# Splitting the first attention units of each layer across key ranges, in a four-layer attention kernel on one Trainium2 core

## The chip, the cores and the metric

The kernel runs on one NeuronCore of a Trainium2 chip. The metric is the device time of one launch in microseconds (us). A single-core run has no second die to be compared with, so the granted TensorE clock that each run lists (its mean over the run, as a share of full speed) is used here to tell like runs from unlike ones; all runs below carry the state "fast".

## The reference

Four layers of self-attention with residual, without a feed-forward part; layers 0 and 2 use the weights A, layers 1 and 3 the weights B. Each layer's keys and values need the output of the whole layer below.

```python
def _A_ref(x, wqkv, wo):                      # _B_ref is the same
    B, S, D = x.shape                         # 1, 2048, 448
    H = 16; Dh = D // H                       # 16 heads of 28
    qkv = (x @ wqkv).reshape(B, S, 3, H, Dh).transpose(2, 0, 3, 1, 4)
    q, k, v = qkv[0], qkv[1], qkv[2]
    p = _softmax(jnp.einsum("bhqd,bhkd->bhqk", q, k) * Dh ** -0.5, axis=-1)
    o = jnp.einsum("bhqk,bhkd->bhqd", p, v)
    return o.transpose(0, 2, 1, 3).reshape(B, S, D) @ wo

x = A_x
x = x + _A_ref(_layernorm(x), A_wqkv, A_wo)
x = x + _B_ref(_layernorm(x), B_wqkv, B_wo)
x = x + _A_ref(_layernorm(x), A_wqkv, A_wo)
x = x + _B_ref(_layernorm(x), B_wqkv, B_wo)
```

## The kernel before

The 2048 rows are four chunks (`NQC`) of four 128-row tiles (`TPC`). A **unit** is one chunk of 512 queries times one group of four heads; a layer has 16 units. A unit has 16 **steps**, one for each key tile: two score tiles (each two matmuls into a 128x1024 slot of PSUM, the buffers that matmuls write to), two exponentials on ScalarE, and one PV accumulation (the probabilities times V, added up over the key tiles).

```python
for step in range(nstep):                 # 256 steps a layer
    mk_exp(2 * step)                      # ScalarE, 128x1024
    mk_scores(2 * step + 2)               # TensorE
    js.step(W1)                           # up to 440 ns of filler
    mk_exp(2 * step + 1)
    mk_scores(2 * step + 3)
    mk_pv(step)
    js.step(W2)                           # up to 260 ns of filler
    if kt == NT - 1: unit_end(u)          # normalise, transpose
```

Everything else is **filler**: chains of small stages (`ln_chain`, `k_chain`, `v_chain`, `q_chain`, the end of a unit, the output projection) that a scheduler, working when the program is built, puts between the attention matmuls by priority and budget. The order in which it puts them is the order of each engine's instruction list. `js.force` emits the rest of a chain at once.

A softmax needs a bound on its scores. Here a per-head bound `beta` is added through spare rows of Q; it needs the maximum of |k|^2 over **all** keys:

```python
def beta_finish(L):
    V(tensor_reduce(kmax2, kmaxp[:, :, :], max))         # all four chunks
    V(tensor_scalar(betav, kmax2, -0.505, c0v, mult, add))
...
# after the last step of a layer
ctx["act_free"] = True
js.flush(fill=lambda: pe_fill(NFBND))      # the rest, one piece at a time
beta_finish(L + 1); q_fixup(L + 1, 0); qmask(...)
```

So no score of layer L+1 can start before the last chunk of layer L is projected, added to x, normalised, and turned into K and its maximum. `pe_fill` issues matmuls whose results are not used.

Of the kernel before, what the change touches and what calls it, by code (L numbers as in the profile page):

```python
# [8 lines left out]
ALU = mybir.AluOpType  # L9
# [210 lines left out]
def build_kernel(nc, A_x, A_wqkv, A_wo, B_x, B_wqkv, B_wo, out,  # L220
                 n_layers=4, c0=50.0, markers=False, NWARM=40, NFPRO=1, NFBND=1, W1=440.0, W2=260.0):
# [18 lines left out]
    with es:  # L240
# [19 lines left out]
        accS = sb("accS", [128, 2, QC], F32)  # L260
        On = sb("On", [128, 2, QC], BF16)
# [11 lines left out]
        kmaxp = sb("kmaxp", [128, G, NQC], F32)  # L273
        kmax2 = sb("kmax2", [128, G], F32)
        betav = sb("betav", [128, G], F32)
# [6 lines left out]
        augrow = sb("augrow", [1, 128], BF16)  # L282
        maskv = sb("maskv", [128, 4], F32)
# [88 lines left out]
        def late_init():  # L372
# [14 lines left out]
        P(lambda g_: g_.affine_select(btmp[:, 0, :], ones_bf[:, 0:128], [[-Dh, 128]], ALU.is_ge, 0.0,  # L387
                                      base=Dh * GW, channel_multiplier=1), reads=["ones_bf", "augrow"], writes=["btmp0"])
        P(lambda g_: g_.affine_select(btmp[:, 1, :], btmp[:, 0, :], [[Dh, 128]], ALU.is_ge, 0.0,
                                      base=Dh - 1 - Dh * GW, channel_multiplier=-1), reads=["btmp0"], writes=["btmp1"])  # L390
        P(lambda g_: g_.affine_select(bsel[:, :], btmp[:, 1, :], [[-1, 128]], ALU.is_ge, 0.0,
                                      base=GW + 3, channel_multiplier=0), reads=["btmp1"], writes=["bsel"])
# [5 lines left out]
        P(lambda g_: g_.tensor_scalar(avec[:, :], maug[:, :], -0.505, None, ALU.mult), reads=["maug"], writes=["avec"])  # L398
        P(lambda g_: g_.affine_select(mtmp2[:, 0:4], ones_f[:, 0:4], [[-Dh, 4]], ALU.is_ge, 0.0,
# [5 lines left out]
        P(lambda g_: g_.tensor_tensor(maskv[:, :], mtmp2[:, 0:4], mtmp2[:, 4:8], ALU.add),  # L405
          reads=["mt2a", "mt2b"], writes=["maskv"])
# [94 lines left out]
        def k_chain(L, c, g):  # L501
# [43 lines left out]
            def bq():  # L545
                b = stt["b"]
                sl2 = pb_alloc()
                T(lambda t_: t_.matmul(PB[:, sl2, :], bsel[:, :], sqb[:, b, :], start=True, stop=True),  # L548
                  reads=[("sq", b), "bsel"], writes=[("PB", sl2)])
                pfree("sq", b)  # L550

                def post():
                    V(lambda v_: v_.tensor_reduce(kmaxp[:, g, c:c + 1], PB[:, sl2, :], AX.X, ALU.max),  # L553
                      reads=[("PB", sl2)], writes=[("kmaxp", g, c)])
                    pb_free(sl2)
                return post
            return [(a1, 432, 0, ("bank",)), (a2, 432, 0, ()), (a3, 216, 2, ("sq",)), (bq, 216, 0, ("bank",))]

        def v_chain(L, tt):
# [17 lines left out]
            def a2():  # L577
# [10 lines left out]
                def post():  # L588
                    ev_copy(VA[:, tt, :].rearrange("p (h e) -> p h e", e=HP)[:, :, 0:Dh],
                            PB[:, sl, 0:D].rearrange("p (h d) -> p h d", d=Dh),  # L590
                            reads=[("PB", sl), ("VAone", nb)], writes=[("VA", nb, tt)], prefer_act=False)
                    pb_free(sl)
# [3 lines left out]
        def q_chain(L, c, g, with_beta):  # L596
            ws = L % 2
            cs = c % 2
# [8 lines left out]
            def a1():  # L607
                sl = stt["sl"] = pb_alloc()

                def f(t_):  # L610
                    t_.matmul(PB[:, sl, :], augrow[0:1, :], zrow[0:1, :], start=True, stop=False)  # L611
                    return mm(t_, sl, 0, False)
                T(f, reads=rd + ["augrow", "zrow"], writes=[("PB", sl)])
# [9 lines left out]
            def a3():  # L623
# [3 lines left out]
                def post():  # L627
                    bq_ = stt["bq"] = palloc("qtb")
                    if with_beta:
                        V(lambda v_: v_.tensor_scalar(qtb[:, bq_, :], PB[:, sl, :], betav[:, g:g + 1], None, ALU.add),  # L630
                          reads=[("PB", sl), "betav"], writes=[("qtb", bq_)])
                    else:
                        ev_copy(qtb[:, bq_, :], PB[:, sl, :], reads=[("PB", sl)], writes=[("qtb", bq_)])
                    b = stt["b"] = palloc("sq")
                    if ctx["act_free"]:
                        A(lambda a_: a_.activation(sqb[:, b, :], PB[:, sl, :], ACTF.Square),
                          reads=[("PB", sl)], writes=[("sq", b)])
                    else:
                        V(lambda v_: v_.tensor_tensor(sqb[:, b, :], PB[:, sl, :], qtb[:, bq_, :], ALU.mult),
# [21 lines left out]
        def beta_finish(L):  # L661
            V(lambda v_: v_.tensor_reduce(kmax2[:, :], kmaxp[:, :, :], AX.X, ALU.max),
              reads=[("kmaxp", g, c) for g in range(G) for c in range(NQC)], writes=["kmax2"])
            V(lambda v_: v_.tensor_scalar(betav[:, :], kmax2[:, :], -0.505, c0v[:, 0:1], ALU.mult, ALU.add),
              reads=["kmax2", "c0v"], writes=["betav"])

        def q_fixup(L, g):
            V(lambda v_: v_.tensor_scalar(QT[:, 0, g, :], QT[:, 0, g, :], betav[:, g:g + 1], None, ALU.add),
              reads=[("QT", 0, g), "betav"], writes=[("QT", 0, g)])
# [6 lines left out]
        def spawn_chunk(L, c, prio, vjit, vprio):  # L676
            key = (L, c)
            chunk_cnt[key] = 0

            def done():  # L680
                chunk_cnt[key] += 1
                if chunk_cnt[key] == TPC:
                    for g in range(G):
                        js.add(k_chain(L, c, g), delay=1, prio=prio)
                    for j in range(TPC):
                        js.add(v_chain(L, c * TPC + j), delay=1, prio=vprio + j,
                               tag=("jit", "v", L, c * TPC + j) if vjit else "crit")
# [4 lines left out]
        for c in range(NQC):  # L692
            done = spawn_chunk(0, c, prio=c, vjit=(c >= 2), vprio=c * TPC)
            for tt in range(c * TPC, (c + 1) * TPC):
                js.add(ln_chain(0, tt, done), prio=c)
        js.flush(fill=lambda: pe_fill(NFPRO))
        marker([("KT", 0, 3, NQC - 1)])
        js.add(q_chain(0, 0, 0, False))
        js.flush(fill=lambda: pe_fill(NFPRO))
        beta_finish(0)  # L700
        q_fixup(0, 0)
        qmask(0, 0, 0)
        marker([("QTm", 0, 3)])

        STEPS_PER_UNIT = NT
        SPQ = G * STEPS_PER_UNIT
        UNITS = [(qc, g) for qc in range(NQC) for g in range(G)]
        NSTEP_L = len(UNITS) * STEPS_PER_UNIT
        gt = {"tile": 0, "unit": 0}
# [5 lines left out]
        def layer(L):  # L715
# [5 lines left out]
            assert sorted(pbfree["free"]) == [0, 1, 2, 3], pbfree  # L721
            pbfree["free"] = [2, 3]
            ctx["act_free"] = False
            tb = gt["tile"]
            ub0 = gt["unit"]
            ntile = 2 * NSTEP_L
            lstart = js.now
            lend = lstart + NSTEP_L

            def tinfo(ti):  # L730
                step, hp = divmod(ti, 2)
                u, kt = divmod(step, STEPS_PER_UNIT)
                return u, kt, hp

            def mk_scores(ti):
                u, kt, hp = tinfo(ti)
                qc, g = UNITS[u]
                slot = (tb + ti) % 2
                qb = (ub0 + u) % 2
                if kt == 0 and hp == 0 and u > 0:  # L740
                    js.force(lambda ch: ch.tag == ("jit", "qm", L, u))
# [18 lines left out]
            def mk_pv(step):  # L760
                ti0 = 2 * step
                u, kt, _ = tinfo(ti0)
                qc, g = UNITS[u]
                aslot = (ub0 + u) % 2
                if u == 0:
                    js.force(lambda ch: ch.tag == ("jit", "v", L, kt))

                def f(t_):
                    ins = None
                    for i in range(4):  # L770
# [5 lines left out]
                                        start=(kt == 0), stop=(kt == NT - 1), tile_position=(0, 32 * i))  # L776
# [4 lines left out]
            def unit_end(u):  # L781
                qc, g = UNITS[u]
                aslot = (ub0 + u) % 2
                ub = cnt["ub"] % 2
                cnt["ub"] += 1
                ob = qc % 2
                stt = {}

                def s1():
                    V(lambda v_: v_.tensor_copy(accS[:, ub, :], PB[:, aslot, :]), reads=[("PB", aslot)], writes=[("accS", ub)])  # L790
                    if ctx["act_free"]:
                        pbfree["free"].append(aslot)
# [50 lines left out]
                js.add([(s1, 0, 1, ()), (s2a, 250, 0, ("bank",)), (s2, 250, 1, ()), (s3, 300, 0, ("bank",))], delay=1, prio=js.now)  # L843

            def chunk_tail(qc):
                ob = qc % 2
                c = qc
                done = None if last else spawn_chunk(L + 1, c, prio=lend, vjit=(c == NQC - 1), vprio=lend + c * TPC)
                for j in range(TPC):
# [14 lines left out]
                    def t1(j=j, tt=tt, stt=stt):  # L864
# [10 lines left out]
                        def post():  # L875
# [6 lines left out]
                            else:  # L882
                                js.add(ln_chain(L + 1, tt, done), delay=1, prio=lend)
                        return post
                    js.add([(t0, 380, 1, ("bank",)), (t1, 380, 0, ())], delay=1 + j, prio=js.now + 8)

            for c in range(1, NQC):
                for g in range(G):
                    js.add(q_chain(L, c, g, True), delay=(c - 1) * SPQ + SPQ // 2 + 2 * g, prio=lstart + c * SPQ - 8,
                           tag=("jit", "q", L, c, g))  # L890
            if not last:
                for g in range(G):
                    js.add(q_chain(L + 1, 0, g, False), delay=(NQC - 1) * SPQ + SPQ // 2 + 2 * g, prio=lend - 4)
            if L == 0:
                if n_layers > 1:
                    js.add([(late_init, 0, 0, ())], delay=STEPS_PER_UNIT + 2, tag=("jit", "late"))
                for g in range(1, G):
# [106 lines left out]
```

## Time and profile before

| | before |
|---|---|
| median of runs | 2132.2 us (2129.76 to 2145.55) |
| span of the profiled run | 2128.0 us, mean clock 0.991 |
| ScalarE busy | 92% of the span |
| first exponential starts at | 73.26 us |
| three holes between layers | 28.2 + 33.5 + 27.0 = 88.7 us |
| after the last exponential | 16.5 us |

The page of the kernel before gives busy time by engine, and by group: engine and operation, out <- in, count | busy us, mean ns of one | idle us of the engine just before, and what ended it. PE stands for TensorE's matmuls, PEld for its weight loads, DVE for VectorE, ACT for ScalarE and POOL for GpSimd; L757 is line 757 of the kernel.

```profile
PE 1920.2 (90%) x10474; PEld 574.1 (27%) x10474; DVE 603.3 (28%) x1211; ACT 1967.3 (92%) x2143; POOL 68.4 (3%) x161
...
L757 ACT ACTIVATE PT<-SC 128x1024 bf16<-128x1024 f32 x2048 | 1910.3, 1073 | 55.9 <-PE SC L747 49.4
```

The exponentials fill 1910 of 2128 us. A mean of 1073 ns is not their pace: neighbours overlap, and most start 904 to 921 ns after the one before (917 ns is used as the pitch below). The timeline of ScalarE around the first layer boundary (start, duration, what, count, idle before and its releaser) shows a hole in them:

```profile
558.97 7.55 ACT L757 ACTIVATE PT<-SC 128x1024 bf16<-128x1024 f32 x8
570.15 0.60 ACT L324 ACTIVATE OTn<-PB 128x512 bf16<-128x512 bf16 x1 [3.63 <-PE PB L832]
581.04 1.57 ACT L324 ACTIVATE xnT<-PB 112x512 bf16<-112x512 bf16 x3 [10.30 <-PE PB L487]
...
594.74 5.61 ACT L757 ACTIVATE PT<-SC 128x1024 bf16<-128x1024 f32 x6 [4.04 <-PE SC L747]
```

The exponentials stop at 566.52 and start again at 594.74. The windows view says what each engine did in such a stretch (columns: window, length, then busy us and instruction count of PE, PEld, DVE, ACT and POOL, the granted clock, DMA share, GB/s). Here are the first hole, the second layer, and the second hole:

```profile
566.52:594.74 28.22, 21.05 (x102) 9.27 (x103) 13.15 (x31) 7.11 (x13) 3.43 (x8) 0.94 0.00 1
594.74:1081.28 486.54, 448.54 (x2490) 131.78 (x2488) 143.21 (x283) 477.94 (x512) 9.47 (x24) 1.00 0.00 1
1081.28:1114.74 33.46, 27.35 (x102) 10.83 (x103) 13.43 (x31) 7.15 (x14) 3.43 (x8) 0.74 0.00 0
```

ScalarE, the bottleneck, works 7 us of a hole. TensorE shows 21 us there, but 11 us of that are fill matmuls. The second hole has the same matmuls; it is longer, and the clock fell to 0.74 in it (0.50 from 1095.08 to 1112.14 us).

### The profile page before, as it was taken

The numbers are of one execution on the slowest core, as the hardware profiler recorded it, in microseconds if no ns is written. First come the engines' busy times: TensorE is split into PE (matmuls) and PEld (weight loads), VectorE is DVE, ScalarE is ACT, GpSimd is POOL, SyncE is SP. The second block draws the span as 40 slices with busy tenths as digits, with TensorE's granted clock in tenths as the row PEclk, the third lists the DMA queues.
The fourth block names the chain that finished last, engine by engine and source line by source line (L and its number), as shares of the span: only waits on it lengthen the run. The fifth ranks groups of instructions, "written<-read, shape, count | busy, mean of one in ns | idle before, by whom it ended". The sixth has DMA issues, their size and how long they took to land.

```text
span 2128.0 us, 24673 instructions
## 1 busy us (share of the span) xinstructions
PE 1920.2 (90%) x10474; PEld 574.1 (27%) x10474; DVE 603.3 (28%) x1211; ACT 1967.3 (92%) x2143; POOL 68.4 (3%) x161
## 2 busy tenths in 40 slices
PE   9998999999889898999988999898998888989887
PEld 4322323223222232323222223232322222222222
DVE  5322423323222232423321234232423121212111
ACT  5699999999689999999959999999996999999996
POOL 4000000000000000000000000000000000000000
PEclk9999999999999999999989999999999999999999
DMA  3000000000000000000000000000000000000000
GB/s 88 8 1 1 1 1 1 1 1 1 1 1 1 1 1 1 1 1 1 1 0 1 1 1 1 1 1 1 1 1 0 1 1 9 1 9 1 9 1 9
DMA packets 6606, 8.46 MB, mean 4 GB/s; under 512 B 608, under 2 KB 5600, under 8 KB 6496
## 3 DMA queue, kind: packets, MB, share of 16 engines
q1 hardware_dynamic: 4384, 5.05, 0.9%
q0 software_dynamic: 2112, 1.84, 0.6%
q8 instruction: 82, 1.34, 0.3%
q14 instruction: 28, 0.23, 0.0%
HBM read 5.05 MB, written 1.84 MB: 3 GB/s over the span
## 4 chain that ended last, share of the span: by engine, by line
ACT 58%; PE 37%; DVE 4%; issue 1%; POOL 0%; DVEq 0%; POOLq 0%
ACT PT L757 57%; PE SC L747 16%; PE PB L774 5%; PE PB L510 3%; PE PB L604 3%; DVE On L818 2%; PE SC L332 2%; PE PB L832 1%; PE PB L810 1%; PE PB L517 1%; PE PB L611 1%; DVE rz L815 1%; PE PB L583 1%; PE PB L548 1%; DVE x_sb L876 0%
## 5 line engine op out<-in xcount | busy, mean ns | idle before, releaser
L757 ACT ACTIVATE PT<-SC 128x1024 bf16<-128x1024 f32 x2048 | 1910.3, 1073 | 55.9 <-PE SC L747 49.4
L747 PE MATMUL SC<-QTm,KT 128*128 128x512 bf16 x4096 | 1238.1, 384 | 138.0 <-ACT PT L757 114.4
L747 PEld LDWEIGHTS SC<-QTm,KT 128*128 128x128 bf16 x4096 | 264.4, 98 | 739.8 <-ACT PT L757 640.5
L774 PE MATMUL PB<-PT,VA 128*32 128x512 bf16 x4096 | 410.0, 390 | 5.9 <-ACT PT L757 3.6
L774 PEld LDWEIGHTS PB<-PT,VA 128*32 128x32 bf16 x4096 | 105.2, 92 | 441.3 <-issue 432.4
L790 DVE COPY accS<-PB 128x512 f32<-128x512 f32 x64 | 44.3, 692 | 631.2 <-PE PB L774 631.2
L604 PE MATMUL PB<-xnT,wq 112*112 112x512 bf16 x256 | 92.2, 402 | 0.0
L510 PE MATMUL PB<-xnT,wq 112*112 112x512 bf16 x256 | 85.5, 412 | 0.0
L332 PE MATMUL SC<-ones_bf,ident 128*128 128x512 bf16 x234 | 79.4, 407 | 1.9 <-POOL ident L380 1.9
L876 DVE TENSOR_TENSOR x_sb<-PB,x_sb 128x448 f32<-128x448 f32 x64 | 39.6, 625 | 136.1 <-PE PB L870 136.1
L326 DVE CAST VA<-PB 128x448 bf16<-128x448 f32 x64 | 39.9, 624 | 132.2 <-PE PB L583 132.2
L630 DVE TENSOR_SCALAR qtb<-PB,betav 128x512 bf16<-128x512 f32 x51 | 38.3, 751 | 122.7 <-PE PB L604 122.7
L673 DVE TENSOR_SCALAR QTm<-QT,maskv 128x512 bf16<-128x512 bf16 x256 | 72.8, 348 | 0.1
L815 DVE RECIPROCAL rz<-PB 128x16 f32<-128x16 f32 x64 | 16.5, 258 | 175.9 <-PE PB L810 175.9
L468 POOL TENSOR_SCALAR ve<-mv 128x1 f32<-128x1 f32 x64 | 15.2, 237 | 1544.5 <-DVE mv L467 1544.4
L553 DVE TENSOR_REDUCE kmaxp<-PB 128x1 f32<-128x512 f32 x64 | 42.6, 688 | 74.9 <-PE PB L548 74.9
L832 PE MATMUL PB<-ident,On 128*128 128x128 bf16 x256 | 25.6, 223 | 42.2 <-DVE On L818 42.2
L653 DVE SCALAR_TENSOR_TENSOR QT<-PB,avec,qtb 128x512 bf16<-128x512 f32 x64 | 48.1, 751 | 55.2 <-PE PB L648 54.0
L324 ACT ACTIVATE xnT<-PB 112x512 bf16<-112x512 bf16 x28 | 15.2, 597 | 39.6 <-PE PB L487 39.6
L326 DVE CAST KT<-PB 128x512 bf16<-128x512 f32 x36 | 24.9, 692 | 86.1 <-PE PB L510 86.1
L818 DVE TENSOR_TENSOR On<-PB,rz 128x512 bf16<-128x512 f32 x64 | 44.2, 691 | 2.2
L604 PEld LDWEIGHTS PB<-xnT,wq 112*112 112x112 bf16 x256 | 32.9, 129 | 42.1 <-issue 29.0
(73 smaller groups left out, 824.3 us busy)
## 6 DMA issues: line engine op xcount, KB each, us to landing
out_dram<-x_sb POOLq DMA_DIRECT2D x4, 448.0 KB, 4.3
wq<-in_A_wqkv_dram SPq DMA_DIRECT2D x1, 1176.0 KB, 7.8
wq<-in_B_wqkv_dram SPq DMA_DIRECT2D x1, 1176.0 KB, 13.5
PT<-in_A_x_dram SPq DMA_DIRECT2D x2, 448.0 KB, 6.1
OTn<-in_A_x_dram SPq DMA_DIRECT2D x2, 448.0 KB, 9.4
wop<-in_A_wo_dram SPq DMA_DIRECT2D x16, 24.5 KB
wop<-in_B_wo_dram SPq DMA_DIRECT2D x16, 24.5 KB
```

Of the source, the lines that this page charges most:

```text
L326: V(lambda v_: v_.tensor_copy(out_ap, in_ap), reads=reads, writes=writes)
L332: T(lambda t_, r_=r_: t_.matmul(SC[:, r_ % 2, (r_ // 2 % 2) * 512:(r_ // 2 % 2 + 1) * 512], ident[:, :], ones_bf[:, :], start=True, stop=T ...
L510: return t_.matmul(PB[0:GW, sl, :], wq[ws][:, cc, D + g * GW:D + (g + 1) * GW], xnT[:, cc, c * QC:(c + 1) * QC], start=False, stop=last_)
L604: return t_.matmul(PB[0:GW, sl, :], wq[ws][:, cc, g * GW:(g + 1) * GW], xnT[:, cc, c * QC:(c + 1) * QC], start=False, stop=last_)
L653: V(lambda v_: v_.scalar_tensor_tensor(QT[:, cs, g, :], PB[:, sl2, :], avec[:, 0:1], qtb[:, bq_, :], ALU.mult, ALU.add), reads=[("PB", sl2 ...
L673: V(lambda v_, i=i: v_.tensor_scalar(QTm[:, qb, i, :], QT[:, cs, g, :], maskv[:, i:i + 1], None, ALU.mult), reads=[("QT", cs, g)] + maskk, ...
L747: ins = t_.matmul(SC[:, slot, j * 512:(j + 1) * 512], KT[:, g, kt * 128:(kt + 1) * 128], QTm[:, qb, i, :], start=True, stop=True)
L757: A(lambda a_: a_.activation(PT[:, pslot, :], SC[:, slot, :], ACTF.Exp, scale=SCALE), reads=[("SC", slot)], writes=[("PT", pslot)], name=" ...
L774: ins = t_.matmul(PB[32 * i:32 * i + 32, aslot, :], VA[:, kt, h * HP:(h + 1) * HP], PT[:, pslot, j * 512:(j + 1) * 512], start=(kt == 0), ...
L790: V(lambda v_: v_.tensor_copy(accS[:, ub, :], PB[:, aslot, :]), reads=[("PB", aslot)], writes=[("accS", ub)])
L818: V(lambda v_: v_.tensor_tensor(On[:, ub, :].rearrange("p (a e) -> p a e", e=HP), PB[:, sl, :].rearrange("p (a e) -> p a e", e=HP), rz[:, ...
L832: ins = t_.transpose(pv_[:, s_ * 128:(s_ + 1) * 128], On[:, ub, s_ * 128:(s_ + 1) * 128], ident[:, :])
```

## The change

Its intent: start the next layer without its last key chunk. Four things belong to it.

1. The first four units of a layer (query chunk 0, all four head groups) run keys 0-11 first (parts A, 12 steps each), then keys 12-15 (parts B). The accumulator of part A is parked in SBUF and added at the end of B. The last chunk thus has 48 steps (96 exponentials, about 88 us) to arrive in.
2. `beta` comes from the first three chunks. If the last chunk has a larger key, its K gets a lowering term through a second set of spare rows, and its V a compensating factor `fv` (a small exponential on ScalarE).
3. The flush between layers goes; the last unit's end becomes filler, and so do the projection, layer norm and K of the last chunk, tagged `("late", L + 1)` and forced only before the first part B.
4. In the prologue the first exponential waits for three chunks and not four.

```diff
+            for u in range(nsp):
+                subs.append((u, list(range(0, KTA)), "A"))
+            for u in range(nsp):
+                subs.append((u, list(range(KTA, NT)), "B"))
+            for u in range(nsp, len(UNITS)):
+                subs.append((u, list(range(NT)), "F"))
 ...
+                if kt == kts[0] and hp == 0:
+                    js.force(lambda ch: ch.tag == ("jit", "qm", L, si))
+                    if kind == "B" or (kind == "F" and si == 2 * nsp):
+                        js.force(lambda ch: ch.tag == ("late", L))
 ...
+        def late_fix(L):
 ...                                   # s0: key difference, added to K of the last chunk
+            def s1():
+                sl = stt["sl"] = pb_alloc()
+                T(matmul(PB[:, sl, 0:H], ones_bf, dtab))
+                def post():
+                    V(tensor_copy(fvt, PB[:, sl, 0:H]))
+                    A(activation(fv, fvt, Exp, scale=-SCALE))
+                    pb_free(sl)
+                    for tt in range(c3 * TPC, (c3 + 1) * TPC):
+                        js.force(lambda ch, tt=tt: ch.tag == ("jit", "v", L, tt))
+                        V(tensor_tensor(VA[:, tt, :], VA[:, tt, :], fv, mult))
+                return post
 ...
+            def k_done():
+                kdone[L] = kdone.get(L, 0) + 1
+                if kdone[L] == (NQC - 1) * G:
+                    js.add([(lambda: beta_prime(L), 0, 0, ())], prio=prio - 1, tag=("jit", "beta", L))
+                    for g in range(G):
+                        js.add(q_chain(L, 0, g), delay=0, prio=prio - 1, tag=("jit", "q", L, 0, g))
 ...                                   # V chains of a chunk: prio=prio + 1
-            ctx["act_free"] = True
-            js.flush(fill=lambda: pe_fill(NFBND))
-            if not last:
-                beta_finish(L + 1)
-                q_fixup(L + 1, 0)
-                qmask(0, 0, gt["unit"] % 2)
```

(Set-up of masks and buffers is left out, and so are smaller moves, such as Q masks made three steps before their unit in place of five.)

## The prediction

> **What bounds the kernel now.** ScalarE's softmax exponentials: the page's groups give 2048 exp ACTIVATEs (128x1024), union busy 1910 us of a 2128 us span. The ScalarE timeline gives a pitch of 0.92 us in a quiet stretch (24 in 22.28 us), and five holes in which no exp runs:
> - prologue: first exp at 73.26 us;
> - three layer boundaries, last exp to first exp: 566.5-594.7 (28.2), 1081.3-1114.7 (33.5), 1602.1-1629.1 (27.0), together 88.7 us: a serial chain of the last unit's transposes, output projection, layer norm, last chunk's K, key maximum, beta, Q mask. The middle one had a granted clock of 0.75 (windows view);
> - tail: 16 us.
>
> Within a layer 512 exps take 492.7, 486.5, 487.3 and 482.8 us: TensorE filler costs little (the last layer has less and is only 4 us shorter); each unit end leaves a 0.45 us hole.
>
> **What the change does.** The first four units run key tiles 0-11 first, then 12-15. The last chunk's tail, layer norm, K and V become filler behind 48 steps (96 exps, about 88 us). Beta comes from the first three chunks; a correction factor goes into the last chunk's K and V.
>
> **Removed.** Each boundary hole shrinks to one pipeline refill: last exp, its PV (0.40 us), two score matmuls (0.4 to 0.6): about 1.2 us. From the prologue the fourth chunk's layer norm and K go (chunk 2's K ends near 51 us, chunk 3's near 66); in the built order chunk 2's layer norm precedes chunk 1's K. After the last Square some 7.5 us of chain stay. First exp near 54 us: 19 saved.
>
> **Added, per layer.**
> - The moved filler: a chunk with filler loses some 2 us more than one without; about 2.5, plus 0.5 for the last unit's hole.
> - The correction: a small exp (128x16) that waits for a VectorE copy, which waits for a TensorE matmul behind two score matmuls. It stands in ScalarE's order, so the next big exp waits too[...]; three forced V tiles behind it on TensorE (0.76 us each, from the prologue's pairs) add 1.[...]
> - Four more sub-unit changes (copy 0.69 us, masks 4 x 0.35 us on VectorE, 28% busy): 0.5.
>
> So 6.5 to 7.5 us a layer with the refill; the first about 6 (it takes in the fourth chunk's work).
>
> **Sum.** 54 + layers 499 + 494 + 494 + 490 + tail 16 = 2047 us span; times run 2 to 4 us above the span (2132.2 against 2128): **2051 us**, range **2036 to 2073**. Faster by over 2%: 0.95; within: 0.04; slower: 0.01.
>
> **What would show it.** ScalarE gaps of 1 to 2 us at the boundaries; first exp near 54 us; a gap of 1 to 2 us around each small exp; half-clock stretches at boundaries gone; exp busy near 1910 us; layer stretches 490 to 499 us; tail unchanged.
>
> **What would make it wrong.** VectorE's queue blocked behind the late chain, delaying Q masks or the K fix and stalling scores; correction stalls of several us;[...] a first layer much slower with the displaced work. All would leave gaps in the first 150 us of a layer.

The forecast's sum came to 2047 us of span and 2051 us of time. The wait at the correction's small exponential, which the author put at 1.3 us a layer, is cut. The 6.5 to 7.5 us a layer and the sum contain it: 1.2 + 2.5 + 0.5 + 1.3 + 1 + 0.5 = 7.0. Measured, that wait costs 1.20 us, and that the next exponential starts behind the small one is seen under fv_later.

## More of the kernel before

The kernel before was run again beside each set.

Filler shares two spare PSUM banks; the other two of four hold the PV accumulation.

## The result, and the profile after

| | before | after |
|---|---|---|
| median of runs | 2132.45 us (16 runs) | 2065.24 us (8 runs, 2062.65 to 2074.44) |
| ratio | | 0.9683, 95% interval 0.9661 to 0.9706 |

A ratio here is the mean time of one kernel's fast runs over that of the other's of the same rounds, so it is not quite the ratio of the medians.

The changed kernel has two kinds of run: most at 2062.7 to 2065.3 us with a mean clock of 0.996 to 0.999, some at 2074.4 us with 0.990. The first profile caught the second kind (span 2072.3 us). The control run below is the same kernel, and its profile caught the first kind (span 2061.3 us); "after" means that profile unless said otherwise. Its page:

```profile
PE 1870.5 (91%) x10351; PEld 564.1 (27%) x10351; DVE 677.5 (33%) x1393; ACT 1945.6 (94%) x2096; POOL 69.9 (3%) x172
...
L872 ACT ACTIVATE PT<-SC 128x1024 bf16<-128x1024 f32 x2048 | 1915.7, 1065 | 68.3 <-PE SC L862 61.0
```

The exponentials are as busy as before (1916 us); VectorE has 74 us more to do. The first boundary, ScalarE timeline:

```profile
555.78 9.38 ACT L872 ACTIVATE PT<-SC 128x1024 bf16<-128x1024 f32 x10
566.19 6.62 ACT L872 ACTIVATE PT<-SC 128x1024 bf16<-128x1024 f32 x7 [1.03 <-PE SC L862]
```

The hole of 28.2 us is now 1.03 us. On TensorE's timeline the 1.03 us is one PV, which waits for the last exponential, and the first scores behind it:

```profile
565.22 0.40 PE L889 MATMUL PB<-PT,VA 128*32 128x512 bf16 x4 [0.90 <-ACT PT L872]
565.55 1.04 PE L862 MATMUL SC<-QTm,KT 128*128 128x512 bf16 x4
```

Where the time went, as differences of spans, in stretches from one layer's first exponential to the next layer's:

| stretch | before | after | difference |
|---|---|---|---|
| prologue, to the first exponential | 73.26 | 59.12 | -14.1 |
| layer 0 with its boundary | 521.48 | 507.07 | -14.4 |
| layer 1 with its boundary | 520.00 | 496.60 | -23.4 |
| layer 2 with its boundary | 514.39 | 496.60 | -17.8 |
| layer 3 with the tail | 498.91 | 501.86 | +2.9 |
| span | 2128.04 | 2061.25 | -66.8 |

So 85.6 us of holes went (88.7 less 3 x 1.03), and 14.1 us of prologue; some 33 us came back inside the layers (85.6 + 14.1 - 66.8 = 32.9). The experiments first ask whether the hidden boundary is the cause, and then where the 33 us are.

### The profile page after: what moved, and what is told of

The parts are those of the page before. It is cut to its first block, busy times and chain, and to the rows that moved or that the text cites. A ratio compares the mean times of both kernels' runs of the same rounds, so it can differ in the third digit from the quotient of the medians.

```text
span 2072.3 us, 24611 instructions
## 1 busy us (share of the span) xinstructions
PE 1882.7 (91%) x10351; PEld 567.0 (27%) x10351; DVE 677.9 (33%) x1393; ACT 1946.3 (94%) x2096; POOL 69.7 (3%) x172
## 4 chain that ended last, share of the span: by engine, by line
ACT 54%; PE 38%; DVE 5%; issue 1%; POOL 1%; DVEq 0%; ACTq 0%; POOLq 0%
ACT PT L872 54%; PE SC L862 18%; PE PB L889 6%; PE PB L642 3%; PE PB L542 3%; DVE On L942 2%; PE PB L956 1%; PE PB L934 1%; PE PB L649 1%; PE PB L549 1%; DVE rz L939 1%; PE PB L617 1%; PE PB L606 1%; DVE qtb L674 0%; PE PB L580 0%
## 5 line engine op out<-in xcount | busy, mean ns | idle before, releaser
L862 PEld LDWEIGHTS SC<-QTm,KT 128*128 128x128 bf16 x4096 | 271.4, 99 | 684.1 <-ACT PT L872 570.7
L916 DVE COPY accS<-PB 128x512 f32<-128x512 f32 x48 | 33.2, 692 | 424.4 <-PE PB L889 424.4
L674 DVE TENSOR_SCALAR qtb<-PB,betav 128x512 bf16<-128x512 f32 x63 | 47.3, 751 | 161.3 <-PE PB L642 161.3
L642 PE MATMUL PB<-xnT,wq 112*112 112x512 bf16 x256 | 93.5, 407 | 0.0
L750 DVE TENSOR_SCALAR QTm<-QT,maskv 128x512 bf16<-128x512 bf16 x320 | 90.8, 348 | 0.1
L337 DVE CAST KT<-PB 128x512 bf16<-128x512 f32 x52 | 36.0, 692 | 134.5 <-PE PB L542 134.5
L939 DVE RECIPROCAL rz<-PB 128x16 f32<-128x16 f32 x64 | 16.5, 258 | 167.6 <-PE PB L934 167.6
L500 POOL TENSOR_SCALAR ve<-mv 128x1 f32<-128x1 f32 x64 | 14.3, 224 | 1520.6 <-DVE mv L499 1520.6
L642 PEld LDWEIGHTS PB<-xnT,wq 112*112 112x112 bf16 x256 | 33.3, 130 | 43.3 <-issue 30.6
L677 DVE TENSOR_TENSOR sqb<-PB,qtb 128x512 bf16<-128x512 f32 x63 | 43.6, 692 | 2.2
L542 PEld LDWEIGHTS PB<-xnT,wq 112*112 112x112 bf16 x256 | 32.0, 129 | 39.0 <-issue 26.3
```

Of the source, the lines that this page charges most:

```text
L337: V(lambda v_: v_.tensor_copy(out_ap, in_ap), reads=reads, writes=writes)
L542: return t_.matmul(PB[0:GW, sl, :], wq[ws][:, cc, D + g * GW:D + (g + 1) * GW], xnT[:, cc, c * QC:(c + 1) * QC], start=False, stop=last_)
L642: return t_.matmul(PB[0:GW, sl, :], wq[ws][:, cc, g * GW:(g + 1) * GW], xnT[:, cc, c * QC:(c + 1) * QC], start=False, stop=last_)
L674: V(lambda v_: v_.tensor_scalar(qtb[:, bq_, :], PB[:, sl, :], betav[:, nb, g:g + 1], None, ALU.add), reads=[("PB", sl), ("betav", nb)], wr ...
L677: V(lambda v_: v_.tensor_tensor(sqb[:, b, :], PB[:, sl, :], qtb[:, bq_, :], ALU.mult), reads=[("PB", sl), ("qtb", bq_)], writes=[("sq", b)])
L750: V(lambda v_, i=i: v_.tensor_scalar(QTm[:, qb, i, :], QT[:, cs, g, :], maskv[:, i:i + 1], None, ALU.mult), reads=[("QT", cs, g)] + maskk, ...
```

## The experiments

### a0_after_again: the control

The changed kernel without an edit.

> The changed kernel unmodified, as the control of this set and to get a profile in its common state: the first profile had a clock of one half for some 30 us in the first layer and ran 2074 us, most runs 2063 to 2065 us with a mean clock of 0.997. Expected 2064 us; in a profile of that state the first 50 us of exponentials should lose about 10 us less than in the first profile, and all later layers (496.6, 496.6, 486.3 us) should be the same to 0.5 us.

Measured: correct, median 2064.33 us (2063.34 to 2074.45, 6 runs) beside 2130.94 us before; ratio 0.9686 (0.9658 to 0.9713). Its first 32 exponentials lose 10.1 us against a pitch of 917 ns; in the first profile they lose 20.8 us. Layers 1, 2 and 3 agree between the profiles to 0.1 us. What makes the other 10 us is seen at v_ahead.

### late_flush: the boundary is not hidden

```diff
+            if L > 0:
+                ctx["act_free"] = True
+                js.flush(only=lambda ch: ch.tag == "crit" or ch.tag == ("late", L),
+                         fill=lambda: pe_fill(1))
+                ctx["act_free"] = False
             mk_scores(0)
             mk_scores(1)
```

> Split, correction and short prologue kept, but at each layer boundary the last chunk's tail, layer norm, K and correction are flushed before the first score, with fill matmuls, as the kernel before did. Theory (the gain is the boundary work hidden behind the first parts of four units): three holes of about 30 us come back, each with some 5 us of correction and forced V in series, against some 4 us less filler in each layer: 2064 + 3 x 30 = about 2150 us, slower than the kernel before. Rival (the gain comes from the missing fill matmuls, from half-clock stretches that follow a pause, or from the prologue): under 2100 us.

Measured: correct, median 2165.44 us (4 runs), ratio 1.0152 (1.0123 to 1.0182): slower than before the change. The ScalarE timeline of this run at the first boundary:

```profile
565.09 8.46 ACT L872 ACTIVATE PT<-SC 128x1024 bf16<-128x1024 f32 x9
...
600.57 0.22 ACT L736 ACTIVATE fv<-fvt 128x16 f32<-128x16 f32 x1 [3.86 <-DVE fvt L735]
608.24 1.94 ACT L872 ACTIVATE PT<-SC 128x1024 bf16<-128x1024 f32 x2 [7.45 <-PE SC L862]
```

The holes are 34.7, 37.3 and 37.5 us. With split, correction and shorter prologue all in place, showing the boundary costs 101 us. The rival is out: the gain comes from hiding this chain; without that, the split, the correction and the shorter prologue together only cost. The holes are longer than the 30 us expected: after the small exponential of the correction 7.45 us more pass before the first score is there, and I had put the whole correction at 5 us.

### nsplit1, nsplit2, nsplit3: how much time the split must buy

```diff
-                 ... W1=440.0, W2=260.0, NSPLIT=4, KTA=12):
+                 ... W1=440.0, W2=260.0, NSPLIT=1, KTA=12):    # 2 and 3 in the others
 ...
-                        js.force(lambda ch: ch.tag == ("late", L))
+                        while any(ch.tag == ("late", L) for ch in js.chains):
+                            js.force(lambda ch: ch.tag == ("late", L))
```

The loop is needed because a forced chain spawns the next one (layer norm, then K, then the correction), which a single pass doesn't see. With four splits nothing is left to force, so the changed kernel never meets this; with one split its single pass lets scores read keys not yet written.

> Only one unit is split in place of four, so 12 steps (22 us) stand between the boundary and the first key of the last chunk; what is not done by then is forced at once. Theory (the split buys time for a serial chain that takes about 31 steps in the stream): after 12 steps projection and part of the layer norm are done, the rest (layer norm, K, maximum, correction) comes back as a hole of 15 to 20 us in each of the layers 1 to 3, and about 12 us in the first: 2064 + 65 = about 2130 us. Rival (any overlap of the boundary is enough, as long as scores can start): under 2085 us.

> Two units split: 24 steps, between the 12 that brought back holes of 29 us a layer and the 36 that brought none. In the control the late chain of layers 1 to 3 has two of its four K blocks done by step 24 and ends at step 29 (33 in the first layer). Theory (what is not done by the deadline runs as one serial piece): holes of about 10 us in layers 1 to 3 and about 14 us in the first: 2064 + 44 = about 2108 us, between 2064 and 2186. Rival (a few forced jobs cost only their own matmul time): under 2080 us.

> Three units split in place of four: 36 steps. In the control the correction is issued at step 29 of layers 1 to 3 and at step 33 of the first, so all is still done in time, nothing is forced, and one sub-unit change a layer is saved. Theory: 2061 to 2065 us, the same as the control or 1 to 2 us less. If chain and deadline are tighter than the order of issue says, holes show at the first key of the last chunk and the time rises by over 5 us.

| units split | steps before the first late key | median | ratio to before |
|---|---|---|---|
| 1 | 12 | 2185.78 us (4 runs) | 1.0246 (1.0214 to 1.0277) |
| 2 | 24 | 2124.59 us (4 runs) | 0.9948 (0.9917 to 0.9980) |
| 3 | 36 | 2065.10 us (6 runs) | 0.9693 (0.9665 to 0.9722) |
| 4 (control) | 48 | 2064.33 us (6 runs) | 0.9686 (0.9658 to 0.9713) |

All were correct. ScalarE in layer 1 with one unit split:

```profile
611.25 12.04 ACT L874 ACTIVATE PT<-SC 128x1024 bf16<-128x1024 f32 x13
650.80 0.22 ACT L736 ACTIVATE fv<-fvt 128x16 f32<-128x16 f32 x1 [27.51 <-DVE fvt L735]
650.92 1.01 ACT L874 ACTIVATE PT<-SC 128x1024 bf16<-128x1024 f32 x1
656.88 3.77 ACT L874 ACTIVATE PT<-SC 128x1024 bf16<-128x1024 f32 x4 [4.95 <-PE SC L864]
```

This settles what the split does: it buys steps for a serial chain that takes about 30 of them. Past that, more split is worth nothing (3 against 4); below it, what is left comes back as a hole. I mis-sized the holes twice: 27.5 + 5.0 us in layer 1 with one split (expected 15 to 20), 9.1 + 5.0 us with two (expected about 10). A forced chain is slower than a flushed one: it runs one K block wholly before the next, so every hand-over between engines is paid, and a lower clock came with it (mean 0.97 with one split, 0.98 with two). In layer 1 of nsplit1, a run with a mean clock of 0.969, a K block starts every 4.5 us; in the flush before layer 1 of late_flush the evictions of K follow each other at 1.5 to 3.1 us. So what was left of the chain after 12 steps still cost 32.5 us, against 34.7 us for all of it there. That nsplit1 is even slower than late_flush comes from layer 0, where late_flush has no deadline to miss: 541 us against 514 us within that layer.

### fv_later: the correction's small exponential

In the changed kernel the correction runs like this in layer 1 (all engines; lines left out):

```profile
621.17 0.60 PE L862 MATMUL SC<-QTm,KT 128*128 128x512 bf16 x2
...
622.08 0.60 PE L862 MATMUL SC<-QTm,KT 128*128 128x512 bf16 x2
...
622.52 0.17 PE L730 MATMUL PB<-dtab,ones_bf 128*128 128x16 bf16 x1
...
622.76 0.18 DVE L735 COPY fvt<-PB 128x16 f32<-128x16 f32 x1
...
622.97 0.21 ACT L736 ACTIVATE fv<-fvt 128x16 f32<-128x16 f32 x1 [0.94 <-DVE fvt L735]
...
625.97 6.59 ACT L872 ACTIVATE PT<-SC 128x1024 bf16<-128x1024 f32 x7 [0.96 <-PE SC L862]
```

The small exponential takes 0.216 us. But it stands in ScalarE's order, so ScalarE waits 0.94 us for a copy that waits for a matmul behind scores. The next exponential waits too: its scores (621.17) are done at 621.77, and it starts at 623.09, behind the small one (622.97). The second gap, 0.96 us, comes from three V tiles forced onto TensorE in the same place. The edit issues the exponential (and the V scaling) one step later:

```diff
+            def s2():
+                A(activation(fv, fvt, Exp, scale=-SCALE))
+                for tt in ...:  force V, scale V        # was in the post of s1
-            return [(s0, 0, 1, ()), (s1, 60, 0, ("bank",))]
+            return [(s0, 0, 1, ()), (s1, 60, 1, ("bank",)), (s2, 0, 0, ())]
```

> The small correction exponential is issued to ScalarE one step (two exponentials) later than the VectorE copy that feeds it; nothing is left out. Theory: ScalarE takes its work in order and the 1.15 us that it idles before the small exponential (4.6 us in four) is waiting, not work. Then the idle before it is under 0.3 us and the pitch over it falls from 2.1 us to about 1.2 us; the forced V tiles remain (1 us). Time 3 to 5 us under the control. Rival: the loss there is TensorE's, from the three forced V tiles, and the time moves under 1.5 us.

Measured: correct, median 2066.58 us (6 runs), ratio 0.9685 (0.9658 to 0.9713). The median says nothing, since three of the six runs were of the slower-clock kind. The profile does:

```profile
633.39 0.27 ACT L740 ACTIVATE fv<-fvt 128x16 f32<-128x16 f32 x1
633.50 2.00 ACT L874 ACTIVATE PT<-SC 128x1024 bf16<-128x1024 f32 x2
...
636.75 5.68 ACT L874 ACTIVATE PT<-SC 128x1024 bf16<-128x1024 f32 x6 [1.26 <-PE SC L864]
```

The wait before the small exponential is gone, as the theory says. The forced V tiles now stand in one block and cost 1.26 us in place of 0.96. The 32 exponentials around it lose 2.55 us in place of 3.29: 0.73 us a layer, 2.9 us in all, which is also the difference of the best runs at clock 0.999 (2059.73 against 2062.65). That is just under the 3 to 5 us expected; both causes, the wait and the forced V, were there.

### q_after_v: a half-done accumulation holds a PSUM bank

The largest loss that I had not foreseen is in the next to last unit of layers 0 to 2 (the expectation below counts them 1 to 3): its 32 exponentials lose 6.57 us, those of the same unit before the change about 1.7 us. All engines in that stretch of the control (lines left out):

```profile
994.82 0.42 PE L642 MATMUL PB<-xnT,wq 112*112 112x512 bf16 x1
...
995.28 0.75 DVE L674 TENSOR_SCALAR qtb<-PB,betav 128x512 bf16<-128x512 f32 x1 [2.88 <-PE PB L642]
996.06 0.69 DVE L677 TENSOR_TENSOR sqb<-PB,qtb 128x512 bf16<-128x512 f32 x1
...
996.81 0.39 PE L649 MATMUL PB<-ones_bf,augrow 1*128 1x512 bf16 x1 [1.14 <-DVE sqb L677]
...
998.02 1.02 ACT L872 ACTIVATE PT<-SC 128x1024 bf16<-128x1024 f32 x1 [1.28 <-PE SC L862]
```

One Q block's last matmul (L642), VectorE's two instructions on its bank, and only then the first matmul of the next Q block (L649), which waits for the second of them: they use the same bank. The scores behind L649 in the order of issue start after it, at 997.39, and ScalarE idles 1.28 us. The order of issue tells why two spare banks don't help. When the third chunk's last K is done, the Q chains of the next layer are added with priority `prio - 1`, ahead of V with `prio + 1`. In the built order one V chain has just issued its first two matmuls and then gets no budget for 15 steps; until it ends it keeps a spare bank. TensorE's timeline of the control shows both halves of that V chain (L606, then L617), 34 us apart with all four Q chains between them:

```profile
988.01 0.54 PE L606 MATMUL PB<-wq,xnT 112*128 112x448 bf16 x2
...
1022.18 0.54 PE L617 MATMUL PB<-wq,xnT 112*128 112x448 bf16 x2
```

The edit:

```diff
-                        js.add(q_chain(L, 0, g), delay=0, prio=prio - 1, ...)
+                        js.add(q_chain(L, 0, g), delay=0, prio=prio + 2 if L else prio - 1, ...)
```

> One number changed: the next layer's first Q chains get a priority behind that chunk's V instead of ahead of K and V. In the changed kernel's profile the unit next to last of layers 1 to 3 loses 6.6 us against 1.7 us of its like before the change: TensorE stands before a Q matmul until VectorE has read the same PSUM bank. Theory: a half-done V accumulation holds one of the two spare banks for 15 steps, so the Q chains follow each other through the other one. Then V is finished first, that unit loses about 2 us, and the time falls by 3 x 4.5 = 13 us, to about 2051 us. Rival: four Q chains at once are too much for VectorE (each 1.4 us of eviction), whatever the banks; then the loss stays near 6 us wherever they are put, and the time stays within 3 us of the control.

Measured: correct, median 2051.82 us (6 runs, 2046.99 to 2059.61), ratio 0.9622 (0.9594 to 0.9649): 12.5 us under the control's median, and 15.7 us between the best runs of each kernel at clock 0.999 (2046.99 against 2062.65, which is from the first call of the changed kernel). The unit loses 1.6 us. For the first matmul of a Q block, the view of that line lists in the control what its idle time ended with (us, times):

```profile
  issue: 21.0, 50
  DVE sqb L677: 16.6, 12
```

and in this run:

```profile
  issue: 26.1, 62
  DVE kmaxp L585: 0.4, 1
```

The 16.6 us of waiting for VectorE are gone, with the same Q chains and the same VectorE work. The chains were not spread out either: the four take 25 us (1003.8 to 1029.1) in this run and 29 us (991.7 to 1020.8) in the control, and the V chain's halves are now 3.6 us apart (982.95 and 986.50). So it is the bank and not VectorE's load. A scheduler can thus undo the use of two banks by leaving one group half done: here that is the 16.6 us.

### v_ahead: forced V tiles in the first layer, and the clock

In the first layer V tiles that are late are forced just before the PV that reads them. TensorE in the control:

```profile
74.95 0.54 PE L617 MATMUL PB<-wq,xnT 112*128 112x448 bf16 x2
76.21 0.40 PE L889 MATMUL PB<-PT,VA 128*32 128x512 bf16 x4 [0.72 <-DVE VA L337]
```

```diff
-                js.force(lambda ch: ch.tag == ("jit", "v", L, kt))
+                for kv in kts[:kts.index(kt) + 2]:
+                    js.force(lambda ch, kv=kv: ch.tag == ("jit", "v", L, kv))
```

> In the first layer V tiles that are not there in time are forced right before the PV matmul that reads them, and in the control's profile TensorE then stands 0.72 us before that PV until VectorE has written the tile (five times). Here a V tile is forced one key tile earlier; nothing else moves. Theory: TensorE's place in its order, not the V work, costs that time; the first 32 exponentials lose about 10 us in the control and should lose 5 to 6 us, so 4 us less in all, 2060 us. If these stops are also what lets the clock fall to one half in the first layer (in the 2074 us runs), no run should be over 2068 us. Rival: the matmul work of the forced tiles itself is the loss (0.76 us a tile); then under 1.5 us is won.

Measured: correct, median 2060.05 us (5 runs, 2056.74 to 2060.89), ratio 0.9652 (0.9626 to 0.9679). In its profile the PV of that place starts without a wait:

```profile
73.66 0.54 PE L617 MATMUL PB<-wq,xnT 112*128 112x448 bf16 x2
74.13 0.40 PE L890 MATMUL PB<-PT,VA 128*32 128x512 bf16 x4
```

The first 32 exponentials lose 7.9 us in place of 10.1 (5 to 6 were expected), and the first layer takes 503.9 us in place of 507.1. The gain in the median, 4.3 us, is as expected. The profile's 3.2 us is too little, since the two profiles are not alike: this one has 6.8 us at half clock from 60.3 us on, right after the first exponential, and the control's has none there. Runs of equal mean clock differ by 5.2 us (0.996: 2060.1 against 2065.3) and 5.9 us (0.999: 2056.74 against 2062.65). So the waits cost 5 to 6 us; how much of what is left is the V work itself, no run shows.

The slower-clock runs are the second finding. In the first profile of the changed kernel (windows view):

```profile
81.40:84.80 3.40, 1.73 (x10) 0.44 (x8) 1.94 (x3) 1.81 (x2) 0.00 (x0) 1.00 0.00 0
84.80:88.20 3.40, 3.21 (x8) 1.14 (x9) 2.02 (x6) 0.81 (x2) 0.00 (x0) 0.55 0.00 0
88.20:105.00 16.80, 14.65 (x46) 4.02 (x44) 4.76 (x7) 6.09 (x7) 0.00 (x0) 0.50 0.00 0
```

TensorE is busy 1.73 of 3.40 us, in the stretch of these waits, and then runs at half clock for some 20 us. (This profile also has 10 us at half clock from 57.8 us on. nsplit3's has the 20 us alone, and its first 32 exponentials lose 17.9 us, so the 20 us cost 7.8 of the 10.7 us.) Of the 33 runs of the five variants that keep these waits and the short prologue with at least three splits (the changed kernel twice, q_after_v, fv_later, nsplit3), 12 have a mean clock of 0.994 or less. Of the 16 runs of v_ahead and the two combined kernels below, none has; the lowest is 0.995. The waits and the half clock thus go together. Why only a third of the runs show it can be read from the traces. In each of them the stretches at half clock, if the end of the run doesn't cut them, are multiples of 3.41 us long (10.24 and 20.48 us, three and six, in the first profile; 6.83, 3.41 and 17.07 in the one before the change), so a run can be laid out in steps of 3.41 us; and all six profiles that keep the waits have a dip, 3.41 us with TensorE busy 1.56 us. Where one step takes in most of the dip, the 20 us of half clock follow: TensorE is busy 1.56 us of that step in the first profile, 1.57 in fv_later, 1.70 in nsplit3 and 1.65 in late_flush. In the control and q_after_v the dip falls on two steps (2.15 and 2.25 us; 2.07 and 2.25 us), and the clock stays. In v_ahead, comb and comb_tr2 no 3.41 us between 62 and 100 us have under 3.1 us busy. So in these nine profiles the waits make the dip, and the half clock came only where one step took in most of it. That its place decides whether it costs is inferred from them; no run set the steps.

### full_pro and pro_no_fix: the prologue part undone

```diff
         crit0 = lambda ch: ch.tag == "crit" or ch.tag == ("jit", "beta", 0) or ch.tag == ("jit", "q", 0, 0, 0) \
-            or (... ch.tag[:3] == ("jit", "v", 0) and ch.tag[3] < TPC)
+            or ch.tag == ("late", 0) \
+            or (... ch.tag[:3] == ("jit", "v", 0) and ch.tag[3] < 2 * TPC)
```

> The prologue part of the change is undone: the fourth chunk's layer norm, K and correction, and four more V tiles, are done before the first exponential again, as before the change; the boundaries stay as changed. Theory from the two profiles: the first exponential goes back from 59.1 to about 73.5 us (14.5 us later), but the first layer then loses 8 to 10 us less, since that work no longer stands in its stream: 2068 to 2071 us, so the prologue's net share of the gain is about 5 us of 67. Rival: the moved work is hidden fully, and 14 us are lost: 2078 us.

Measured: correct, median 2087.49 us (6 runs), ratio 0.9785 (0.9759 to 0.9812). This missed the expectation. The first layer did take 8.8 us less (498.3 against 507.1), as expected; but the first exponential started at 85.5 us and not at 73.5, so this run does not restore the prologue before. (The profile is of the fastest of the six runs; the other five have a mean clock of 0.992 to 0.994.) The second try keeps the correction in the stream, by giving it a tag of its own in layer 0:

```diff
-                    js.add(late_fix(L), ..., tag=("late", L))
+                    js.add(late_fix(L), ..., tag=("late", L) if L else ("fix", 0))
```

> The prologue part undone a second time, because the first try delayed the first exponential to 85.5 us: there the first unit's Q masks stood on VectorE behind the first layer's correction (key fix, four V tiles and their scalings), which the kernel before does not have. Here the fourth chunk's layer norm and K and four V tiles are back in the prologue, but the correction stays in the stream. Theory: first exponential at 73 to 76 us (73.3 before the change); the first layer's pitch loses about 33 us in place of 39 (the first try: 30); time about 2071 us, so the prologue's net share of the gain is 5 to 9 us. If the first exponential still starts after 80 us, the order of the fill, not the correction, made the first try late.

Measured: correct, median 2081.76 us (5 runs), ratio 0.9759 (0.9745 to 0.9772). Another miss. The ScalarE timelines of the two tries, full_pro and then pro_no_fix:

```profile
77.21 0.22 ACT L736 ACTIVATE fv<-fvt 128x16 f32<-128x16 f32 x1 [4.52 <-DVE fvt L735]
85.45 1.94 ACT L873 ACTIVATE PT<-SC 128x1024 bf16<-128x1024 f32 x2 [8.03 <-PE SC L863]
```

```profile
81.36 5.68 ACT L873 ACTIVATE PT<-SC 128x1024 bf16<-128x1024 f32 x6 [4.24 <-PE SC L863]
```

In pro_no_fix 81.4 us are left; the last four K blocks are evicted 2.85 us apart in that profile, those of the chunk before 1.54 us apart. By what I had set down, the order of the fill and not only the correction makes both tries late. So no run isolates the prologue's share. An estimate from the profiles is small: 14.1 us earlier, less the 8.8 us that the same work costs in the stream, about 5 us. The two runs show only that putting it back into the changed kernel's order costs 17 to 23 us.

### comb and comb_tr2: the repairs together

comb takes q_after_v, v_ahead and fv_later, and spreads the four V scalings, two steps each, so that V tiles have been issued as ordinary filler by then:

```diff
-            return [(s0, 0, 1, ()), (s1, 60, 0, ("bank",))]
+            return [(s0, 0, 1, ()), (s1, 60, 1, ("bank",)), (s2, 0, 1, ())] + \
+                [(lambda tt=tt: s3(tt), 0, 2, ()) for tt in range(c3 * TPC, (c3 + 1) * TPC)]
```

comb_tr2 also mends something that both kernels have. TensorE before the change, at the end of a unit:

```profile
1057.39 0.40 PE L832 MATMUL PB<-ident,On 128*128 128x128 bf16 x4 [0.65 <-DVE On L818]
1057.63 0.59 PE L747 MATMUL SC<-QTm,KT 128*128 128x512 bf16 x2
```

The unit's last transpose waits 0.65 us for VectorE's normalisation, the scores behind it start at 1057.63, and ScalarE loses 0.45 us. The edit issues that transpose one step later:

```diff
-                js.add([(s1, 0, 1, ()), (s2a, 250, 0, ("bank",)), (s2, 250, 1, ()), (s3, 300, 0, ("bank",))],
+                js.add([(s1, 0, 1, ()), (s2a, 250, 0, ("bank",)), (s2, 250, 2, ()), (s3, 300, 0, ("bank",))],
```

> The changed kernel with three orders of issue mended and no work taken out: Q chains behind V (13 us measured alone), forced V tiles one key tile earlier (4 us measured alone), and the correction's small exponential one step later with its four V scalings spread over the next steps, so that no V tile is forced there (0.7 us a layer was won by the later exponential alone; the forced V cost 1.3 us a layer more, so 4 x 1.8 = 7 us). Additive: 2064 - 13 - 4 - 7 = 2040 us. If they share one cause the sum falls short: over 2046 us.

> As the one before, with one thing more that the profiles of both kernels show: at nearly every unit end one exponential pitch is 1.475 us in place of 0.92, because TensorE stands in its order before the last transpose of the unit until VectorE has normalised. Here that transpose is issued one step later. Theory: the hole goes: 60 unit ends x 0.45 us = 27 us, so about 2013 us. Rival: the stop only moves to the next matmul in the order or the later transpose delays what follows; then under 8 us.

Measured, both correct: comb 2035.35 us (6 runs, 2034.24 to 2036.49), ratio to before 0.9538 (0.9513 to 0.9562); comb_tr2 1999.58 us (5 runs, 1998.16 to 2002.24), ratio 0.9372 (0.9347 to 0.9396). comb is 29 us under the control (24 were expected), also between runs of equal mean clock (0.996: 2036.3 against 2065.3). So the repairs add up: at equal clock the three alone won 15.7, 5.2 to 5.9 and 2.9 us, and the rest, about 5 us, is left for spreading the V scalings, which no run has alone. comb_tr2 wins 35.8 us more where 27 were expected: I had counted 0.45 us at 60 unit ends, but a unit with little filler lost 0.64 us before and 0.08 after, so 0.56 us at 64 of them, which is 36 us. (The two profiles differ by 34.1 us.) The ScalarE timeline of layer 1 in the control

```profile
673.45 7.54 ACT L872 ACTIVATE PT<-SC 128x1024 bf16<-128x1024 f32 x8 [0.45 <-PE SC L862]
681.45 7.54 ACT L872 ACTIVATE PT<-SC 128x1024 bf16<-128x1024 f32 x8 [0.45 <-PE SC L862]
```

becomes one stretch in comb_tr2:

```profile
639.42 120.87 ACT L877 ACTIVATE PT<-SC 128x1024 bf16<-128x1024 f32 x129
```

## Why the prediction was right, and where it was off

It said 2051 us with a range of 2036 to 2073; 2065 us was measured, a gain of 67 us where 81 were predicted; the slower-clock runs, at 2074.4 us, lie just outside the range. Cause and direction were right, and late_flush shows the cause. Term by term, in span us:

| term | predicted | measured | difference |
|---|---|---|---|
| to the first exponential | 54 | 59.1 | +5.1 |
| layer 0 | 499 | 507.1 | +8.1 |
| layer 1, layer 2 | 494 each | 496.6 each | +5.2 |
| layer 3 | 490 | 486.2 | -3.8 |
| tail | 16 | 15.7 | -0.3 |
| sum | 2047 | 2061.3 | +14.3 |

- **"Each boundary hole shrinks to one pipeline refill ... about 1.2 us"**: right. 1.03 us at each of three boundaries, and the half-clock stretches there are gone.
- **The correction: the wait, put at 1.3 us, and "1" for the forced V**: right. The pitch over the small exponential is 2.12 us and the one two later 1.98 us, against 0.917 us: 1.20 + 1.06 us.
- **Exponentials near 1910 us busy, tail unchanged**: right (1916 us; 15.7 against 16.5 us).
- **"First exp near 54 us"**: mis-sized by 5.1 us. In the first profile of the changed kernel four V casts stand on VectorE at 28.1 to 31.3 us, ahead of the rest of chunk 1's layer norm, and its first K eviction is at 37.3 us, against 32.8 us before the change. I had read off the built order that chunk 2's layer norm comes sooner and not asked what comes later. This is read from the traces; no run tested it.
- **"the first about 6"** for the loss of layer 0: mis-sized by 8 us. The Q chains on one bank are 5.1 of them (502.0 us in q_after_v's profile; see the next point). The forced V tiles, for which TensorE waits (0.72 us, five times in the control), are 5.2 to 5.9 more (v_ahead, runs of equal clock), so the rest of the layer's filler came out 2 to 3 us under. In a third of the runs a half clock adds some 10 us more; that one I had looked for at the boundaries alone.
- **Layers 1 and 2**: the sum came out 2.6 us short each, but it hides a miss. The Q chains that share one bank cost 5.1 us in each of the layers 0 to 2 (layer 1 takes 491.5 us in q_after_v against 496.6), which I had not seen; other filler was cheaper than I had put in. That half of the miss cancels is luck. I had named VectorE's queue as what could go wrong. It was TensorE's queue, behind a PSUM bank.
- **Layer 3** was 3.8 us better than predicted: it grew from 482.4 to 486.2 us where some 7 us had been added. The correction is 2.3 of those, so the moved filler and the sub-unit changes cost about 1.5 us together, less than set down for them.

What stays open: the prologue's exact share, since both attempts to undo it also changed the order of the fill; and the smaller moves of the change, such as the later Q masks, which no run has alone.

## What to carry to other kernels

A serial chain between two phases can be hidden by reordering the next phase so that the part which needs the chain comes late, but count the chain's length in the stream and give it at least that many steps: 36 steps were as good as 48, 24 lost nearly all of the gain, and 12 were worse than no split. After such a change look for the new waits in the engines' orders: here an instruction queued too soon (a small exponential, a transpose, a V tile right before its reader) or an accumulation left half done in one of two PSUM banks cost 65 us together (36 of them before the change as well), and all of it came back by changing the order of issue alone. Filler that fits in busy time still costs when it stands in front of the bottleneck's next operand: three forced V tiles made ScalarE wait 0.96 us in layer 1 of the control.
